# Attention output with both pairs' left-over keys first, GpSimd waits on VectorE, and a plan with other durations

## The chip, the cores and the metric

One core of a Trainium2 chip runs the whole kernel. The metric is the device time of one execution in microseconds (us), as the median of several runs. Engine names are those of the profile: PE (TensorE), PEld (its weight loads), DVE (VectorE), ACT (ScalarE), POOL (GpSimd), SP (SyncE, which issues the DMAs).

## What is computed

For 8 batches, 12 heads, 448 positions and a head width of 64, attention with normalized queries and keys, then a gated MLP on the heads laid side by side:

```python
q_n, k_n = rmsnorm(q, g_q), rmsnorm(k, g_k)
scores = q_n @ k_n.T / sqrt(64)
attn = exp(scores - max) ; attn /= sum + 1e-9
x = (attn @ v) laid out as (8, 448, 768)
h = gelu(x @ w_in)                  # 768 -> 1024, u and v halves of 512
v_n = layernorm(v) * g_ln
v_s = w_sg @ v_n + b_sg             # over the 448 positions
out = x + (u * v_s) @ w_out         # 512 -> 768
```

Inputs are float32; the kernel splits most operands into a high and a low 16-bit half (names ending in `h` and `l`) and adds three products of halves for each product.

## The kernel before

**The work.** Two heads are a pair, two pairs (`NG = 2`, index `j`) are a unit `u`; there are 24 units, three to a batch. For a unit, `split` (L740) normalizes queries and keys on POOL, DVE and ACT (tiles `qk`, `hl`) and a transposing DMA makes `qt`. `scores` (L793) forms seven score tiles `s`, each of 12 matmuls in 64x64 weight tiles; DVE takes the row extremum (`jk`), ACT the exponential (`ex`), ACT or DVE the two halves (`ahl`), and a transposing DMA writes them to `at`. [...]

**The attention output** is `pv` (L855). It runs twice per unit (`e = 0, 1`: four and three of the unit's seven query chunks), 48 times in all, and adds into one PSUM tile `pv`. 448 keys are three whole chunks of 128 and a left-over of 64. `steps` (L859) lists both: the left-over keys take two weight tiles of 64x64, a whole chunk two tiles of 128x64. With the three products of halves this makes 12 blocks per pair, and `blocks` is ordered with the three left-over blocks first. The loop runs over the pairs outside and the blocks inside, so that the left-over blocks of pair 1 come after the whole chunks of pair 0, and it yields after block 5 of each pair and after pair 0. `recips` (L828) takes the reciprocals of the sums on POOL and DVE (`rx`, `ry`, `rh`, `rl`), `rows` (L839) spreads them by matmuls of 128x64, and DVE multiplies.

**The MLP** (`moe`, L905) uses whole 128x128 weight tiles (`mv`, `mu`, `ms`, `mo`); its instructions are recorded with an offset `MOFF` in their priority.

**What sets the order.** No engine call is made directly. A `Tape` records each as a task with a priority (the place in which it was recorded, plus an offset), a duration from `cost` (L127) and what it depends on. On PE consecutive matmuls of one output tile and one weight-tile shape are one task, and a `yield` cuts a task. `schedule` (L247) then plans all engines together in time, an available task with the lowest priority number first; for PE it charges a change of the weight-tile shape (`SWITCH`) and may prefer a task of the present shape that is up to `HYST` places later. [...] Some tasks may go to either of two engines (`either`, L226). `emit` (L403) writes the tasks in the planned order of start, so each engine's queue has that order; at run time the engines wait for data and buffers alone. All instructions are issued on L425, so the profile tells them apart by tile.

Of the kernel before, what the change touches and what calls it, by code (L numbers as in the profile page):

```python
# [15 lines left out]
ALU = mybir.AluOpType  # L16
# [5 lines left out]
LEAST = 1.125 * 2.0 ** -15  # L22
ASC = 2.0 ** 14


MOFF, MOFF0, GP = 340, 100, 350

HI, EL, LO, SQ, QH, QL, RW, XH, OT, GH, VH = "A", "VA", "V", "A", "AV", "G", "A", "A", "A", "A", "A"

# [22 lines left out]
SWITCH, HYST = (133, 92), 160  # L52
BIAS = dict(A=0, V=0, G=0)
SLACK = (0, 0)
OVER, PATIENCE = dict(V=130, G=150), 300
START = dict(T=60, A=34, V=33, G=85, S=28, N=0)


class Tile:
# [37 lines left out]
class Tape:  # L97

    def __init__(self, tc):
        self.tc, self.tiles, self.tasks, self.off, self.count = tc, {}, [], 0, 0  # L100
        self.after = set()
        self.grouped = self.last = None
        self.masks, self.swap = {}, None

    def free(self, ap):
        n = 1
# [20 lines left out]
    def cost(self, q, op, a, kw):  # L127

        aps = [x for x in kw.values() if isinstance(x, bass.AP)]
        n = max([self.free(x) for x in aps], default=1)  # L130
        wide = [k for k in ("in_", "in0", "in1") if k in kw and self.free(kw[k]) > max(n // 2, 1)]
        psum = any(self.tiles[kw[k].tensor.name].pool.space for k in wide if kw[k].tensor.name in self.tiles)
        if q.eng == "T":
            t, big = kw["lhsT"], kw["rhs"]
            rows, cols = (64 if ap_n <= 64 else 128 for ap_n in (t.shape[0], self.free(t)))
            m = self.free(big)
            d = max(m / 2.4, 26.7 if cols == 64 else 53)
            if big.dtype == F32R:
                d = max(d, 186)
            if big.dtype == F32:  # L140
                d = max(4 * m / 2.4, 250)
            return d * rows * cols / 128 ** 2 + (4 if rows == cols == 128 else 3), 170, (rows, cols)
        if q.eng != "S" and "dma" in op:
            return 700, 4000, None
        if q.eng == "S":
            b = n * kw["out"].shape[0] * mybir.dt.size(kw["out"].dtype)
            if "transpose" in op:
                return 1530, b / 458752, True
            return 600, b / 220e3, False
        if "preload" in op:  # L150
            return 1283, 0, None
        if q.eng == "A":
            ptr = sum(isinstance(kw.get(k), bass.AP) for k in ("bias", "scale"))
            return 0.833 * n + (70 if psum else 100) + 80 * ptr + (200 if "accum_out" in kw else 0), 100, None
        if q.eng == "V":
            if op == "reciprocal":
                return 70 + 6.5 * n, 75, None
            ptr = sum(isinstance(kw.get(k), bass.AP) for k in ("scalar", "scalar1", "scalar2"))
            one = len(wide) == 1 and not psum and "reduce" not in op and "bn" not in op
            f32 = one and (mybir.dt.size(kw[wide[0]].dtype) == 4 or kw[wide[0]].dtype == U16)  # L160
            return (0.52 if f32 else 1.04) * n + 75 + 40 * ptr + (70 if "accum_out" in kw else 0), 75, None
        if n < 100:
            return 1.5 * n + 185, 20, None
        wide = [k for k in wide if len([x for x in kw[k].ap if x[0]]) == len(kw[k].ap)]
        return (1.86 if len(wide) > 1 else 2.5 if op == "tensor_scalar" else 1.64) * n + 210, 20, None

    def port(self, q, op, kw):

        if q.eng == "G":
            return True  # L170
        if q.eng != "V" or max(self.free(v) for v in kw.values() if isinstance(v, bass.AP)) < 16 or op not in ("tensor_tensor", "scalar_tensor_tensor", "tensor_scalar", "tensor_copy"):
            return False
        aps = [v for v in kw.values() if isinstance(v, bass.AP) and v.tensor.name in self.tiles]
        return not any(self.tiles[v.tensor.name].pool.space for v in aps)
# [72 lines left out]
    def schedule(self):  # L247
# [42 lines left out]
        T = self.tasks  # L290
# [7 lines left out]
        free = dict.fromkeys(START, 0.0)  # L298
# [7 lines left out]
        mode, dma, left, now, port = None, (0.0, False), len(T), 0.0, 0.0  # L306
        while left:
            moved = True
            let_go()
            while moved:  # L310
                moved = False
                for e in START:
# [5 lines left out]
                    t, put = None, []  # L318
                    while avail[e] and t is None:
# [6 lines left out]
                        shared = T[k].alts[e][3] if T[k].alts else T[k].port  # L326
# [4 lines left out]
                        t = T[k]  # L331
                    if e == "T" and t is not None and t.mode != mode:
                        same = [x for x in avail[e] if T[x[1]].mode == mode and x[0] < t.prio + HYST and opens(T[x[1]], now)]
                        if same:
                            x = min(same)
# [3 lines left out]
                            t = T[x[1]]  # L339
# [19 lines left out]
                    if t.port:  # L359
                        over = min(OVER[e], occ / 2)  # L360
                        port = max(port, now + over) + occ - over
# [4 lines left out]
                    end = free[e] + t.lat  # L366
                    if e == "S":
                        z, x = t.lat, max(0.0, dma[0] - now)
                        if t.mode:
                            occ += min(1350, max(0, 0.85 * (x - 1750)))  # L370
                            end = max(now + 2500 + 1550 * z, min(now + 3000 + 1750 * z, dma[0] + 2400 * z), dma[0] + 1520 * z)
                        else:
                            occ += 450 * (dma[1] and x > 2000)
                            end = max(now + 2500 + 400 * z, dma[0] + (1000 if dma[1] else 500) + 400 * z)
# [8 lines left out]
                            heapq.heappush(events, tl.end)  # L383
                    for s in succ[t.id]:
                        f = T[s].eng
                        r = free[e] + 15 if f == e and not T[s].alts else end + START[f]
                        ready[s] = max(ready[s], r)
                        need[s] -= 1
                        if not need[s]:
                            for f in T[s].alts or (f,):  # L390
                                heapq.heappush(later[f], (ready[s], s))
                            heapq.heappush(events, ready[s])
# [10 lines left out]
    def emit(self, real_pools):  # L403
        tc = self.tc

        def real(v):
            tl = self.tiles.get(v.tensor.name) if isinstance(v, bass.AP) else None
            if tl is None:
                return v
            if tl.real is None:  # L410
                shape, dtype = tl.args
                tl.kw.pop("kind", None)
                tl.real = real_pools[tl.pool.name].tile(list(shape), dtype, **tl.kw)
            r = tl.real if v.dtype == tl.real.dtype else tl.real.bitcast(v.dtype)
            return bass.AP(tensor=r.tensor, offset=v.offset, ap=v.ap)

        for t in self.schedule():
            for c in t.calls:
                if t.eng == "N":
                    real_pools["swap"]()  # L420
                    continue
                q, op, a, kw = c
                kw = {k: real(v) for k, v in kw.items()}
                first = (kw.pop("out"),) if op == "memset" else ()
                getattr(q.nc_eng, op)(*first, *a, **kw)  # L425


@with_exitstack
def kernel(
# [15 lines left out]
    B, H, S, D = q.shape  # L445
# [8 lines left out]
    HP = P // 2  # L454
# [5 lines left out]
    NG = 2  # L460
# [17 lines left out]
    V, A, G = nc.vector, nc.scalar, nc.gpsimd  # L478
# [25 lines left out]
    T, A, V, G, SP = (Queue(tape, e, x) for e, x in zip("TAVGS", (nc.tensor, nc.scalar, nc.vector, nc.gpsimd, nc.sync)))  # L504
    mm = T.matmul
# [56 lines left out]
    def decode(dst, raw, most=None):  # L562

        hi, lo = raw[:, :, 1], raw[:, :, 0]
        di = dst.bitcast(I32)
        V.tensor_scalar(out=di, in0=hi, scalar1=0x7FFFFFFF, scalar2=None, op0=ALU.bitwise_and)
        if most is None:
            V.tensor_scalar(out=dst, in0=dst, scalar1=LEAST, scalar2=None, op0=ALU.max)
        else:
            V.tensor_scalar(out=dst, in0=dst, scalar1=LEAST, scalar2=None, op0=ALU.max, op1=ALU.max, accum_out=most)  # L570
        V.tensor_scalar(out=di, in0=di, scalar1=3, scalar2=0x3FFFFFF8, op0=ALU.logical_shift_left, op1=ALU.bitwise_and)
        V.scalar_tensor_tensor(out=di, in0=hi, scalar=-0x40000000, in1=di, op0=ALU.bitwise_and, op1=ALU.bitwise_or)
        V.scalar_tensor_tensor(out=di, in0=lo, scalar=29, in1=di, op0=ALU.logical_shift_right, op1=ALU.bitwise_or)
# [107 lines left out]
    R, U = {}, {}  # L681
# [173 lines left out]
    def pv(u, e):  # L855
        n = C4 - e
        at = U[u]["at"][e]
        av = at.rearrange("p x (c j q) -> p x j c q", j=NG, q=HP)
# [5 lines left out]
        yield  # L864
        ps = ps_m.tile([P, 512], F32, name="pv", tag="pv")[:, 0:n * P]
        pc = ps.rearrange("p (c j q) -> p j c q", j=NG, q=HP)
        for j in range(NG):
            r = R[NG * u + j]
            for k_, (v_, o, hx) in enumerate(blocks):
                for h, (ks, c) in enumerate(hx):  # L870
                    mm(out=pc[h * HP:(h + 1) * HP, j], lhsT=r[v_][ks, c], rhs=av[ks, o + c, j, 0:n],
                       start=(j == 0 and k_ == 0), stop=(j == NG - 1 and k_ == len(blocks) - 1), skip_group_check=True)
                if k_ == 5:
                    yield
            if j == 0:
                yield
        if ROWP:
            row = rows(e, *r_)
# [260 lines left out]
    for i in range(NI + 1):  # L1139
        b, g = divmod(i, NP)  # L1140
        u = i // NG
# [92 lines left out]
```

## Time and profile before

| | |
|---|---|
| median of 3 runs | 884.81 us (882.46 to 885.58) |
| the profiled execution, its own time | 881.78 us |
| its span, first to last instruction | 880.0 us |
| busy: PE / PEld / DVE / ACT / POOL | 766.3 / 456.0 / 685.8 / 727.9 / 317.6 us |
| mean granted TensorE clock | 0.957 |

A profile's row for a group names the line, the engine, the instruction, output and input tiles, and how many there are. In a timeline the time from one matmul's start to the next one's is what a matmul occupies PE for; the durations beside them overlap, because matmuls are pipelined.

### The profile page before, as it was taken

To read this page: it belongs to the slowest core of one execution; us is meant where nothing else is said; L and a number is where in the kernel's file an instruction comes from. 1 tells how busy PE (TensorE), PEld (TensorE's weight loads), DVE (VectorE), ACT (ScalarE), POOL (GpSimd) and SP (SyncE) were. 2 spreads that over 40 slices of the span, in tenths; PEclk is the share of its full clock that TensorE was granted. 3 is DMA by queue.
4 is the path that set the end of the run, shared out by engine and by line. 5 is a ranking of instruction groups with operands and counts; after the bars stand their busy time and mean duration, and the time that the engine had idled before them with its cause. 6 is when DMAs were issued, how large, how long until landed. Compare 5 with 4: busy or idle time off the path is not lost.

```text
span 880.0 us, 20978 instructions
## 1 busy us (share of the span) xinstructions
PE 766.3 (87%) x7766; PEld 456.0 (52%) x7766; DVE 685.8 (78%) x1690; ACT 727.9 (83%) x1495; POOL 317.6 (36%) x458
## 2 busy tenths in 40 slices
PE   0445669547999999999999999999999999999997
PEld 0222334223574467544754477456745575457457
DVE  6899997998887987868877979688887978583150
ACT  4779789987988998989999989799999978884351
POOL 3554520274453344535433506542553341000000
PEclk9997869856999999999999999999999999999999
DMA  6999989889899959998999599969999698635002
GB/s 161 262 256 233 227 178 216 162 187 215 167 221 227 204 116 217 231 199 167 188 221 219 129 215 188 226 157 180 210 226 175 124 183 178 147 85 100 19 1 72
DMA packets 433942, 155.96 MB, mean 177 GB/s; under 512 B 402544, under 2 KB 427696, under 8 KB 433840
## 3 DMA queue, kind: packets, MB, share of 16 engines
q1 hardware_dynamic: 433840, 154.63, 85.8%
q8 instruction: 61, 1.00, 0.5%
q14 instruction: 41, 0.34, 0.1%
HBM read 43.57 MB, written 11.01 MB: 62 GB/s over the span
## 4 chain that ended last, share of the span: by engine, by line
PE 56%; DVE 18%; ACT 14%; issue 5%; DMA 3%; POOL 2%; SPq 0%; ACTq 0%; DVEq 0%; POOLq 0%
PE pv L425 11%; PE s L425 8%; DVE jk L425 4%; ACT ex L425 3%; DVE dec L425 3%; ACT ahl L425 3%; ACT L425 2%; PE row L425 2%; DMA at<-ahl 2%; DVE vl L425 1%; DVE ahl L425 1%; DVE ss L425 1%; ACT u L425 1%; POOL qk L425 1%; ACT sqk L425 1%
## 5 line engine op out<-in xcount | busy, mean ns | idle before, releaser
L425 ACT ACTIVATE ex<-s,nm 128x448 int32<-128x448 f32 x336 | 212.3, 634 | 29.8 <-DVE jk L425 25.3
L425 DVE TENSOR_SCALAR_CACHE_REDUCE jk<-s 128x448 bf16<-128x448 f32 x336 | 199.5, 617 | 43.5 <-PE s L425 42.6
L425 PE MATMUL s<-qt 64*64 64x448 f16 x2016 | 148.3, 383 | 79.7 <-ACT ex L425 58.1
L425 ACT ACTIVATE ahl<-ex 128x896 f16<-128x896 uint16 x191 | 179.7, 952 | 8.5 <-DMA at<-ahl 7.8
L425 PEld LDWEIGHTS <-vh 128*64 128x64 f16 (+2 forms) x1792 | 100.5, 111 | 89.7 <-issue 64.0
L425 PE MATMUL pv<-at,vh 128*64 128x256 f16 (+3 forms) x1536 | 140.8, 274 | 5.7 <-DMA at<-ahl 3.1
L425 PEld LDWEIGHTS <-qt 64*64 64x64 f16 x2016 | 62.5, 111 | 117.9 <-issue 76.7
L425 DVE TENSOR_SCALAR ahl<-ex 128x896 f16<-128x896 uint16 x145 | 103.7, 716 | 25.0 <-ACT ex L425 20.7
L425 POOL TENSOR_TENSOR hl<-qk,hl 128x896 f16<-128x896 f32 (+2 forms) x69 | 97.2, 1419 | 21.1 <-DVE hl L425 13.4
L425 POOL TENSOR_SCALAR rx<-sums 128x8 f32<-128x8 f32 (+1 forms) x48 | 16.5, 344 | 213.6 <-ACT ex L425 212.2
L425 POOL TENSOR_TENSOR qk<-qk,ny 128x896 f32<-128x896 f32 x47 | 83.1, 1787 | 1.8
L425 PEld LDWEIGHTS <-wi 128*128 128x128 f16 x576 | 52.0, 98 | 53.0 <-issue 7.7
L425 PE MATMUL pv<-at,vl 128*64 128x192 f16 (+3 forms) x768 | 74.4, 274 | 0.0
L425 PEld LDWEIGHTS <-vl 128*64 128x64 f16 (+2 forms) x896 | 49.3, 110 | 45.0 <-issue 27.7
L425 PEld LDWEIGHTS <-xh 128*128 128x128 f16 (+1 forms) x648 | 48.8, 103 | 42.9 <-issue 18.8
L425 POOL TENSOR_TENSOR qk<-qk,gg 128x896 f32<-128x896 f32 x23 | 48.4, 2106 | 60.3 <-ACT sqk L425 57.2
L425 ACT ACTIVATION_READ_ACCUMULATOR ex<-s,nm 128x1 f32 x336 | 69.0, 205 | 0.0
L425 DVE TENSOR_TENSOR pv<-pv,row 128x512 f32<-128x512 f32 (+1 forms) x48 | 30.2, 629 | 39.5 <-PE pv L425 39.3
L425 DVE TENSOR_REDUCE ss<-sqk 128x14 f32<-128x896 f32 x48 | 51.7, 1079 | 9.2 <-ACT sqk L425 9.1
L425 ACT ACTIVATE sqk<-qk 128x896 f32<-128x896 f32 x48 | 45.7, 954 | 2.9 <-DMA qk<-in_k_dram 1.5
L425 PEld LDWEIGHTS <-xl 128*128 128x128 f16 (+1 forms) x408 | 36.6, 103 | 20.4 <-issue 1.7
L425 ACT ACT_TABLE_LOAD x36 | 46.2, 1283 | 0.6
(1104 smaller groups left out, 1797.7 us busy)
## 6 DMA issues: line engine op xcount, KB each, us to landing
qk<-in_q_dram SPq DMA_DIRECT2D x48, 224.0 KB, 3.8
qk<-in_k_dram SPq DMA_DIRECT2D x48, 224.0 KB, 4.6
out_dram<-ot SPq DMA_DIRECT2D x56, 192.0 KB, 3.2
raw<-in_moe_w_in_dram SPq DMA_DIRECT2D x12, 512.0 KB, 5.3
vr<-in_v_dram SPq DMA_DIRECT2D x32, 192.0 KB, 3.6
vr<-in_v_dram SPq DMA_DIRECT2D x32, 144.0 KB, 3.6
rawo<-in_moe_w_out_dram SPq DMA_DIRECT2D x8, 384.0 KB, 4.0
at<-ahl SPq DMA_TRANSPOSE x168, 4.2
```

What stands on the lines that cost most here:

```text
L425: getattr(q.nc_eng, op)(*first, *a, **kw)
```

## The change

- In `pv` the left-over blocks of both pairs come first (6 blocks), then the whole chunks of pair 0 and of pair 1 (9 blocks each). One loop over the 24 blocks takes the place of two; it yields after blocks 5 and 14 (`CUTS`) and so once less.
- `emit` keeps the last DVE instruction with `port` set. A POOL instruction whose planned duration is over 500 ns (`LONG`) is made to wait for it.
- The plan gets other durations: ACT and DVE constants by some ns, no fast rate for a DVE instruction that also accumulates, and no shared port for it; DVE's latency 85 for 75; between dependent POOL instructions 85 ns for 15 (`AGAIN`). `MOFF` is 300 for 340.
- `decode` is rewritten to record the same instructions.

```diff
-MOFF, MOFF0, GP = 340, 100, 350
+MOFF, MOFF0, GP = 300, 100, 350
+LONG = 500
+CUTS = (5,14)
+CA = 200
+CV = 70
+AG = 85
+AGAIN = dict(T=15, A=15, V=15, G=AG, S=15, N=15)
@@ cost
-            return 0.833 * n + (70 if psum else 100) + 80 * ptr + (200 if "accum_out" in kw else 0), 100, None
+            return 0.833 * n + (52 if psum else 95) + 85 * ptr + (CA if "accum_out" in kw else 0), 100, None
-            one = len(wide) == 1 and not psum and "reduce" not in op and "bn" not in op
+            one = len(wide) == 1 and not psum and "reduce" not in op and "bn" not in op and "accum_out" not in kw
-            return (0.52 if f32 else 1.04) * n + 75 + 40 * ptr + (70 if "accum_out" in kw else 0), 75, None
+            return (0.52 if f32 else 1.04) * n + 70 + 50 * ptr + (CV if "accum_out" in kw else 0), 85, None
@@ schedule
-                        r = free[e] + 15 if f == e and not T[s].alts else end + START[f]
+                        r = free[e] + AGAIN[e] if f == e and not T[s].alts else end + START[f]
@@ emit
-                getattr(q.nc_eng, op)(*first, *a, **kw)
+                ins = getattr(q.nc_eng, op)(*first, *a, **kw)
+                if t.port and q.eng == "V":
+                    holder = ins
+                elif t.port and holder is not None and t.occ > LONG:
+                    tc.add_manual_dep(ins.ins, holder.ins.name, self.behind, reason="shared port")
@@ pv
-        for j in range(NG):
-            r = R[NG * u + j]
-            for k_, (v_, o, hx) in enumerate(blocks):
-                for h, (ks, c) in enumerate(hx):
-                    mm(out=pc[h * HP:(h + 1) * HP, j], lhsT=r[v_][ks, c], rhs=av[ks, o + c, j, 0:n],
-                       start=(j == 0 and k_ == 0), stop=(j == NG - 1 and k_ == len(blocks) - 1), skip_group_check=True)
-                if k_ == 5:
-                    yield
-            if j == 0:
+        steps = [(j, x) for part in (blocks[:3], blocks[3:]) for j in range(NG) for x in part]
+        for k_, (j, (v_, o, hx)) in enumerate(steps):
+            for h, (ks, c) in enumerate(hx):
+                mm(out=pc[h * HP:(h + 1) * HP, j], lhsT=R[NG * u + j][v_][ks, c], rhs=av[ks, o + c, j, 0:n],
+                   start=(k_ == 0), stop=(k_ == len(steps) - 1), skip_group_check=True)
+            if k_ in CUTS:
                 yield
```

**PE, one `pv` tile (the 22nd of 48) before.** `ms` and `mo` are MLP tiles (128x128), `s` a score tile (64x64); `vh_5211`, `vl_5263` are the two halves of pair 0's values, `vh_5281`, `vl_5295` those of pair 1. One row stands for two matmuls (left-over) or for six (whole chunks, 12 for `s`).

```order
L425 MATMUL ms__6124<-ws_h_105,vl_5951 128x448
...
L425 MATMUL pv_6136<-at1_5759,vh_5211 64x3x64
...
L425 MATMUL pv_6136<-at1_5759,vl_5263 64x3x64
...
L425 MATMUL pv_6136<-at1_5759,vh_5211 64x3x64
...
L425 MATMUL ms__6124<-ws_h_105,vh_5945 128x448
...
L425 MATMUL pv_6136<-at1_5759,vh_5211 64x3x64
...
L425 MATMUL pv_6136<-at1_5759,vl_5263 64x3x64
...
L425 MATMUL s_6181<-qt_5232 64x448
...
L425 MATMUL pv_6136<-at1_5759,vh_5281 64x3x64
...
L425 MATMUL pv_6136<-at1_5759,vl_5295 64x3x64
...
L425 MATMUL ms__6206<-ws_h_105,vh_5945 128x448
...
L425 MATMUL pv_6136<-at1_5759,vh_5281 64x3x64
```

Each pair has its own piece of left-over matmuls, and each pair's whole chunks come apart from them.

**The same tile in the change.** Here `vh_5152`, `vl_5180` are pair 0's and `vh_5211`, `vl_5284` pair 1's.

```order
L433 MATMUL ms__6081<-ws_h_105,vl_5940 128x448
...
L433 MATMUL pv_6094<-at1_5807,vh_5152 64x3x64
...
L433 MATMUL pv_6094<-at1_5807,vl_5180 64x3x64
...
L433 MATMUL pv_6094<-at1_5807,vh_5152 64x3x64
...
L433 MATMUL pv_6094<-at1_5807,vh_5211 64x3x64
...
L433 MATMUL pv_6094<-at1_5807,vl_5284 64x3x64
...
L433 MATMUL ms__6081<-ws_h_105,vh_5901 128x448
...
L433 MATMUL pv_6094<-at1_5807,vh_5152 64x3x64
...
L433 MATMUL pv_6094<-at1_5807,vl_5180 64x3x64
...
L433 MATMUL s_6145<-qt_5373 64x448
...
L433 MATMUL pv_6094<-at1_5807,vh_5211 64x3x64
...
L433 MATMUL ms__6185<-ws_h_105,vh_5901 128x448
```

The left-over blocks of both pairs are now one piece of 12 matmuls, and each pair's 18 whole-chunk matmuls stand together; `pv` appears in three pieces where it had five. Over the whole program the shape of the weight tile changes 421 times between one matmul and the next, where it changed 606 times; from the 577th of the 2016 score matmuls on it is 329 for 476.

**POOL, the queries and keys of one unit before,** with the semaphores that each waits for (`DVE_49` is VectorE's).

```order
L425 TENSOR_TENSOR qk_4268<-qk_4268,gg_112 128x896 [waits DMAHW4_49,DMAHW3_49,Activation_49]
...
L425 TENSOR_TENSOR qk_4268<-qk_4268,ny_4968 128x896 [waits DMAHW2_49,DMAHW1_49,Pool_49]
L425 TENSOR_TENSOR qk_4268<-qk_4268,ny_4968 128x896
L425 TENSOR_SCALAR rx_5093<-sums_4813 128x8 [waits Activation_49]
L425 CAST rh_5131<-ry_5118 128x8 [waits DVE_49,PE_49]
L425 TENSOR_TENSOR rl_5133<-ry_5118,rh_5131 128x8 [waits PE_49,Pool_49]
L425 TENSOR_TENSOR hl_5135<-qk_4268,hl_5135 128x2x7x64 [waits DMAHW5_49,DVE_49]
L425 TENSOR_TENSOR hl_5137<-qk_4268,hl_5137 128x2x4x64 [waits DMAHW7_49,Activation_49]
L425 TENSOR_TENSOR hl_5137<-qk_4268,hl_5137 128x2x3x64 [waits DVE_49]
```

Of these wide instructions two wait for DVE.

**The same unit in the change.**

```order
L433 TENSOR_TENSOR qk_4328<-qk_4328,gg_112 128x896 [waits DMAHW4_49,DMAHW5_49,DVE_49,Activation_49]
...
L433 TENSOR_TENSOR qk_4328<-qk_4328,ny_4865 128x896 [waits DMAHW2_49,DMAHW3_49,DVE_49,Pool_49]
L433 TENSOR_TENSOR qk_4328<-qk_4328,ny_4865 128x896 [waits DVE_49]
L433 TENSOR_TENSOR hl_4979<-qk_4328,hl_4979 128x2x7x64 [waits DMAHW6_49,DVE_49,Pool_49]
L433 TENSOR_TENSOR hl_5031<-qk_4328,hl_5031 128x2x4x64 [waits DVE_49]
L433 TENSOR_TENSOR hl_5031<-qk_4328,hl_5031 128x2x3x64 [waits DVE_49,Activation_49]
L433 TENSOR_SCALAR rx_5133<-sums_4886 128x8 [waits Activation_49]
L433 CAST rh_5150<-ry_5145 128x8 [waits DVE_49,PE_49]
L433 TENSOR_TENSOR rl_5154<-ry_5145,rh_5150 128x8 [waits PE_49,Pool_49]
```

Now all of the wide instructions on `qk` and `hl` wait for DVE, and the small `rx`, `rh`, `rl` that `rows` needs stand behind them in the queue. In the whole program 96 of the 138 wide ones wait for DVE, where 31 of 139 did; one multiplication by `ny` has moved to DVE. Casts `hl<-qk` on ACT are 34 where they were 40, on DVE 38 for 32.

## Rows read from the trace of the kernel before

**Rows 1.** The page: busy time by engine, then the span in 40 slices.

```profile
PE 766.3 (87%) x7766; PEld 456.0 (52%) x7766; DVE 685.8 (78%) x1690; ACT 727.9 (83%) x1495; POOL 317.6 (36%) x458
...
PE   0445669547999999999999999999999999999997
...
PEclk9997869856999999999999999999999999999999
```

**Rows 2.** Three stretches: PE, PEld, DVE, ACT, POOL busy; granted clock, DMA share, GB/s.

```profile
0.00:220.00 220.00, 122.90 (x1232) 64.47 (x1232) 196.80 (x461) 178.94 (x352) 89.00 (x123) 0.83 0.98 210
220.00:880.00 660.00, 643.39 (x6542) 391.56 (x6534) 489.02 (x1230) 548.97 (x1143) 228.63 (x335) 1.00 0.82 166
385.00:440.00 55.00, 53.19 (x526) 33.08 (x525) 47.90 (x120) 52.65 (x109) 23.89 (x34) 1.00 0.93 177
```

**Rows 3.** Waits of PE from 220 to 880 us: total us, times, longest.

```profile
PE s L425 <- ACT ex L425: 4.7, 7, 1.0
PE row L425 <- DVE xl L425: 3.1, 5, 1.1
PE pv L425 <- ACT row L425: 2.2, 3, 0.7
```

**Rows 4.** Timeline of PE, 411 to 417 us: start us, us, matmuls.

```profile
411.56 0.27 PE L425 MATMUL pv<-at,vh 64*64 64x192 f16 x2
411.76 0.36 PE L425 MATMUL ms__6124<-ws_h,vh 128*128 128x448 f16 x1
...
412.53 0.35 PE L425 MATMUL ms__6124<-ws_l,vh 128*128 128x448 f16 x1
412.72 0.35 PE L425 MATMUL ms__6124<-ws_h,vl 128*128 128x448 f16 x1
413.00 0.44 PE L425 MATMUL pv<-at,vh 128*64 128x192 f16 x6
413.27 0.41 PE L425 MATMUL pv<-at,vl 128*64 128x192 f16 x6
413.52 0.41 PE L425 MATMUL pv<-at,vh 128*64 128x192 f16 x6
413.90 0.76 PE L425 MATMUL s<-qt 64*64 64x448 f16 x12
414.46 0.28 PE L425 MATMUL pv<-at,vh 64*64 64x192 f16 x2
```

**Rows 5.** DVE groups from 0 to 220 us: busy us, mean ns; idle before.

```profile
L425 DVE TENSOR_SCALAR ahl<-ex 128x896 f16<-128x896 uint16 x21 | 17.2, 821 | 1.2 <-ACT ex L425 1.2
...
L425 DVE SCALAR_TENSOR_TENSOR wr<-rawo,wr 128x384 int32<-128x384 int32 x16 | 12.6, 789 | 0.0
```

**Rows 6.** Timeline of DVE, then of POOL, 191 to 196 us.

```profile
191.52 0.62 DVE L425 TENSOR_SCALAR ahl<-ex 128x896 f16<-128x896 uint16 x1
192.05 2.43 DVE L425 SCALAR_TENSOR_TENSOR wr<-rawo,wr 128x384 int32<-128x384 int32 x1
...
195.94 0.55 DVE L425 SCALAR_TENSOR_TENSOR wr<-rawo,wr 128x384 int32<-128x384 int32 x1
...
191.97 2.10 POOL L425 TENSOR_TENSOR qk<-qk,gg 128x896 f32<-128x896 f32 x1 [1.31 <-ACT sqk L425]
```

**Rows 7.** The chain of waits, 130 to 230 us: start us, us, what.

```profile
192.14 2.34 DVE wr L425
...
197.78 3.73 POOL qk L425 x2
...
214.10 3.43 DVE vl L425 x3
```

**Rows 8.** Timeline of POOL, 394 to 397 us.

```profile
394.36 0.19 POOL L425 CAST rh<-ry 128x6 f16<-128x6 f32 x1
394.51 2.08 POOL L425 TENSOR_TENSOR qk<-qk,gg 128x896 f32<-128x896 f32 x1
396.55 0.38 POOL L425 TENSOR_TENSOR rl<-ry,rh 128x6 f16<-128x6 f32 x1
```

More of the change, by code (lines that the diff above doesn't have):

```diff
@@ L103, in __init__ @@
         self.masks, self.swap = {}, None
+        self.behind = mybir.DependencyInfo(mybir.DependencyClass.Sync, mybir.DependencyReason.SCHED_ONLY)
     def free(self, ap):
@@ L170, in port @@
             return True
-        if q.eng != "V" or max(self.free(v) for v in kw.values() if isinstance(v, bass.AP)) < 16 or op not in ("tensor_tensor", "scalar_tensor_tensor", "tensor_scalar", "tensor_copy"):
+        if q.eng != "V" or "accum_out" in kw or max(self.free(v) for v in kw.values() if isinstance(v, bass.AP)) < 16 or op not in ("tensor_tensor", "scalar_tensor_tensor", "tensor_scalar", "tensor_copy"):
             return False
@@ L415, in real @@
             return bass.AP(tensor=r.tensor, offset=v.offset, ap=v.ap)
+        holder = None
         for t in self.schedule():
@@ L566, in decode @@
         V.tensor_scalar(out=di, in0=hi, scalar1=0x7FFFFFFF, scalar2=None, op0=ALU.bitwise_and)
[L567 to L570, printed above, removed]
+        more = {} if most is None else dict(op1=ALU.max, accum_out=most)
+        V.tensor_scalar(out=dst, in0=dst, scalar1=LEAST, scalar2=None, op0=ALU.max, **more)
         V.tensor_scalar(out=di, in0=di, scalar1=3, scalar2=0x3FFFFFF8, op0=ALU.logical_shift_left, op1=ALU.bitwise_and)
```

## The prediction

> **What bounds the kernel now.** I read the page first, for which engine is full and where. PE is busy 766.3 us of 880, and by slices it has two parts: the first ten slices (to 220 us) are ragged, with a granted clock down to 0.5 in one of them; from 220 us on PE stands at 9 in every slice but the last, at full clock [rows 1]. The windows say the same in us: PE is busy 122.9 of the first 220 us, but 643.4 of the last 660 [rows 2]. A busy PE need not be a useful one, because the ends of matmuls are modelled, so the third view is what PE waits for after 220 us: six entries that come to 12.0 us, the largest of them 4.7 us for ACT's exponentials [rows 3]. POOL is not among them. So for three quarters of the span what PE does one after another is the time. The next engine is ACT: 549.0 of these 660 us, and in the fullest stretch that I looked at 52.7 of 55 us beside PE's 53.2 [rows 2]. Before 220 us the chain goes mainly through DVE and ACT, and DVE is busy 196.8 of 220 us [rows 2].
>
> The fourth view, PE's timeline, shows the price that matters. Inside one shape of weight tile the 128x128 matmuls start 0.19 us apart (412.53 to 412.72); the step from there to `pv`'s 128x64 takes 0.28 us (412.72 to 413.00), 0.09 more. Six whole-chunk matmuls take 0.25 us when the next six have their shape (413.27 to 413.52) and 0.38 us when a score tile of 64x64 follows (413.52 to 413.90), 0.13 more. Coming out of the left-over matmuls into the MLP takes 0.20 us (411.56 to 411.76) where such a pair goes by in about 0.08, 0.12 more. From scores to left-over matmuls, the same shape, a score tile takes just its 0.56 us (413.90 to 414.46) [rows 4]. So a change of shape costs PE 0.09 to 0.13 us; I take 0.11, the middle.
>
> **The change part by part.**
>
> *Order in `pv`.* It removes no matmul. It joins pieces: per `pv` tile one left-over piece for two, and fewer cuts through the whole chunks. The two orders shown above give 606 changes of shape before and 421 now. Of the 185 that go, 38 lie before the 577th score matmul (about 262 us in the profile), where PE is mostly not the bound, and 147 behind it, where it is. 147 x 0.11 = 16.2 us saved; with the two ends of the price 13.2 and 19.1. The 38 early ones (4 us of PE's time) I cost at nothing: the cover is DVE's work, and if that cover is thinner than it looks they add up to 4 us of gain.
>
> *What must keep up.* Joined pieces are longer: a `pv` piece of 18 matmuls takes about 0.8 us (three rows of six), and the order now puts two score tiles one behind the other more often. Both PSUM buffers for scores must then be free at once, or PE stands until ACT has read them. PE waited 4.7 us for that after 220 us [rows 3]. PE also asks for all else 2.5% faster, 16 of 660 us; ACT goes from 549.0 in 660 to about 549 in 644 us, 83% to 85%, less 6 casts that moved to DVE. I add 2 us for waits that come back; the bounds are 0 and 12, which doubles [rows 3].
>
> *GpSimd's waits.* [...] DVE's `wr` took 2.43 us at 192.05 and 0.55 us at 195.94; POOL's multiplication by `gg` had begun at 191.97 and took 2.10 us [rows 6]. DVE lost 1.9 us there, POOL nothing. To 220 us the halves `ahl` average 821 ns on DVE against 0.62 us for one that was not held up, `wr` 789 against 550 [rows 5, 6]: 21 x 0.20 + 16 x 0.24 = 8 us in two forms. Two such stalls lie on the chain itself, the `wr` of 2.34 us and three `vl` of 3.43 us [rows 7], which at 0.55 and 3 x 0.6 would have been 3.4 us less. The new waits let POOL start only behind the DVE instruction that the plan put ahead of it, so some of these stalls go. I take 2 us, near the chain's 3.4 because only stalls on the chain count, and half of it because a held-up DVE instruction that the plan puts behind POOL's is still held up. The gain is bounded by the 8 us of the two forms. The loss: the chain has a POOL piece too, two multiplications of 3.73 us [rows 7]; each can now wait for a DVE instruction of 0.6 us, and a few of those are 2 us. After 220 us I cost the waits at nothing: POOL is busy 228.6 of 660 us and PE's matmuls wait for it nowhere [rows 2, 3].
>
> [...]
>
> *Durations and `MOFF`.* They move work by places, not in amount. One multiplication goes from POOL to DVE at the very start, where both contended anyway. I cost them at nothing; what covers it is that PE's queue holds the same work in nearly the same sequence of units. If a bad place arises it shows as a PE wait, within the 12 us above.
>
> **Sum.** Against the profiled execution's own 881.8 us (span 880.0 and 1.8 around it): 881.8 - 16.2 + 2 - 2 = 865.6, taken as **866 us**. The median of the runs shown stands 3.0 us above the profiled one; carried over to it, the same sum would be 868.6, well within the range.
>
> **The rivals.**
>
> *ACT takes over.* For: in 385 to 440 us it is busy 52.7 of 55 us [rows 2], so there a faster PE finds no scores to work on, and double score tiles bunch its work. Against: over 660 us it has 111 us to spare, and PE's waits for it are short. If half of the stretches give nothing, half of 16.2 is lost: 881.8 - 8.1 + 2 - 2 = 874.
>
> [...]
>
> [...]
>
> *The reciprocals come late (slower).* `rh` and `rl` stand in POOL's queue behind wide instructions. At 394.36 `rh` was followed by a multiplication of 2.08 us, so `rl` began at 396.55 [rows 8]. If now a waiting wide instruction holds such a pair for 2.1 us and PE has nothing else, each costs 2.1 us; the point is 16.2 / 2.1 = 8 of 48 pairs. At 16 pairs the time is 881.8 - 16.2 + 33.6 - 2, about 897. Against: PE's matmuls wait for POOL nowhere after 220 us [rows 3].
>
> *Nothing in the end.* The changes of shape go, and PE waits as much more for data in other places: 880 to 886.
>
> **How the numbers follow.** Forecast (859 to 871, the lock's rival in it) 0.57, of this 0.10 for the lock's rival; ACT takes over (871 to 880) 0.17; startup gives more (848 to 859) 0.12; nothing 0.07; slower 0.07. A range of 850 to 878 holds the forecast, most of the second and third, 0.80 or so; it takes in both ends of the price (863 and 869) and 12 us of waits (876). A measurement of this kernel can tell about 0.5% from no change, that is 4.4 us. Faster by more (under 880.4): 0.57 + 0.17 + 0.12 = 0.86; within: 0.07; slower: 0.07.
>
> **What would show it.** In the profile of the changed kernel, PE's timeline at the same `pv` tile has one left-over piece of 12 matmuls and two of 18, with the starts otherwise at the same pace; PE's waits after 220 us stay near 12 us; the part behind the 577th score matmul is some 16 us shorter. [...] Wrong: PE's waits for `ex`, `rh` or `rl` grow by 10 us or more (ACT or the reciprocals), or 220 us is reached later than now (POOL on the path). If PE's steps at a change of shape stay but their count doesn't pay, the bound was not PE.

## The result

The changed kernel takes **863.14 us** (median of 5 runs, 862.73 to 863.76), the kernel before 882.46 us in the same comparison (881.17 to 885.58): a ratio of 0.977, 95% interval 0.975 to 0.979, 19 us less. The forecast was 866, range 850 to 878. The profiled execution of the changed kernel took 863.8 us (span 862.0), that of the kernel before 881.8; the sum of the forecast against it was 865.6.

The profile after. First the page, busy time and the slices, the answer to [rows 1]:

```profile
PE 745.1 (86%) x7766; PEld 468.1 (54%) x7766; DVE 669.7 (78%) x1696; ACT 721.0 (84%) x1490; POOL 308.6 (36%) x457
...
PE   0445658835999999999999999999999999999997
...
PEclk9998768965999999999999999999999999999999
```

PE is full from the eleventh slice on as before and busy 21.2 us less in all; the granted clock falls below full between the fourth and the tenth slice in both. The windows, columns as in [rows 2]:

```profile
0.00:220.00 220.00, 118.23 (x1235) 67.30 (x1236) 191.71 (x467) 175.24 (x346) 82.57 (x122) 0.83 0.97 206
220.00:862.00 642.00, 626.86 (x6533) 400.80 (x6531) 477.96 (x1230) 545.74 (x1145) 226.03 (x336) 1.00 0.87 173
385.00:440.00 55.00, 54.63 (x599) 36.79 (x597) 44.44 (x115) 51.72 (x115) 20.18 (x32) 1.00 0.90 170
```

PE stays the bound of the long part: it is busy 626.9 of 642.0 us. ACT is at 545.7 of 642.0 (85%), as worked out ahead. PE's waits in that part, as [rows 3]:

```profile
PE s L433 <- ACT ex L433: 4.5, 6, 1.1
PE pv L433 <- ACT row L433: 1.8, 4, 0.7
PE row L433 <- DVE gtl L433: 0.7, 1, 0.7
...
PE row L433 <- POOL rh L433: 0.5, 1, 0.5
```

All ten entries come to 10.1 us, before it was 12.0. The timeline of PE at the `pv` tile whose order stands above, the answer to [rows 4]:

```profile
403.77 0.35 PE L433 MATMUL ms__6081<-ws_l,vh 128*128 128x448 f16 x1
403.96 0.35 PE L433 MATMUL ms__6081<-ws_h,vl 128*128 128x448 f16 x1
404.24 0.27 PE L433 MATMUL pv<-at,vh 64*64 64x192 f16 x2
404.35 0.25 PE L433 MATMUL pv<-at,vl 64*64 64x192 f16 x2
...
404.60 0.24 PE L433 MATMUL pv<-at,vl 64*64 64x192 f16 x2
404.68 0.25 PE L433 MATMUL pv<-at,vh 64*64 64x192 f16 x2
404.86 0.36 PE L433 MATMUL ms__6081<-ws_h,vh 128*128 128x448 f16 x1
...
406.37 0.41 PE L433 MATMUL pv<-at,vl 128*64 128x192 f16 x6
406.61 0.41 PE L433 MATMUL pv<-at,vh 128*64 128x192 f16 x6
406.96 0.76 PE L433 MATMUL s<-qt 64*64 64x448 f16 x12
```

The 12 left-over matmuls are one piece: 0.62 us from its first start to the next MLP matmul (404.24 to 404.86). The steps at a change of shape are what they were: 0.28 us into the piece (403.96 to 404.24) where the pace is 0.19, and 0.35 us for six whole-chunk matmuls ahead of a score tile (406.61 to 406.96) where the six before took 0.24. Only their number fell.

The same price comes out of all of PE's order, and it goes with the shape and not with the cut. I took pieces (consecutive matmuls of one tile and one shape) in the long part, from the first mark of the table below on, and for each the time to the next piece's start less its streaming time, as defined there. In the kernel before the median is 0.135 us at the 502 places where the shape changes and 0.026 us at the 361 places where another tile of the same shape follows; in the changed kernel it is 0.141 us (349) and 0.026 us (326). In these two kernels a cut between pieces of one shape takes 0.026 us; a change of shape takes 0.11 us more.

On DVE beside POOL, the two groups of [rows 5] in the first 220 us:

```profile
L433 DVE TENSOR_SCALAR ahl<-ex 128x896 f16<-128x896 uint16 x22 | 16.2, 734 | 1.8 <-DMA at<-ahl 1.7
...
L433 DVE SCALAR_TENSOR_TENSOR wr<-rawo,wr 128x384 int32<-128x384 int32 x16 | 11.4, 724 | 0.0
```

821 ns became 734 and 789 became 724, where single ones that were not held up took 620 and 550 in [rows 6]: the stalls are fewer, far from gone. In the chain of waits, the answer to [rows 7], the three `vl` that took 3.43 us now take 1.54:

```profile
200.44 1.70 POOL qk L433
...
215.87 1.54 DVE vl L433 x3
```

**One table for all runs.** It is worked out from each trace, PE's matmuls in order of start. Each is given a streaming time in proportion to its columns and to the elements of its weight tile, by which a score tile of 12 gets the 0.56 us of [rows 4], six whole-chunk matmuls 0.24 (406.37 to 406.61), and a 128x128 matmul with 448 columns 0.187, where the timeline's pace is 0.19. A pair of left-over matmuls gets 0.04 where it takes 0.08 (404.60 to 404.68); what is over counts as steps, for the same matmuls in every kernel. The first column is the instant at which 80 us of streaming have started, a fixed amount of work near the end of the ragged part; the second is the rest of the span, with 538 us of streaming in each kernel. What is left of the rest is split: the time from a matmul's start to the next one's, less its streaming time, is added to the steps where it is at most 0.35 us (changes of shape and small losses) and to the gaps where it is more (PE waits). The 5 us that are left follow the last matmul. Medians are of all executions; the other columns are of one profiled execution each. The executions of one kernel spread over 1 us (the changed kernel) to 8 us (run 3), so 1 or 2 us at the first mark show nothing by themselves.

| kernel | runs, median us | to 80 us of streaming | rest | changes of shape in the rest | steps | gaps |
|---|---|---|---|---|---|---|
| before | 882.5 | 227.9 | 652.1 | 502 | 93.5 | 15.7 |
| changed | 863.1 | 226.9 | 635.1 | 349 | 77.4 | 14.7 |
| 1 pv alone | 862.3 | 226.2 | 635.3 | 346 | 76.7 | 15.6 |
| 2 old pv | 875.3 | 227.2 | 645.2 | 494 | 95.4 | 6.4 |
| 3 no waits | 868.7 | 234.3 | 636.1 | 349 | 78.1 | 15.1 |
| 4 waits alone | 876.3 | 226.1 | 649.6 | 502 | 94.0 | 12.7 |
| 5 plan alone | 882.3 | 232.5 | 646.8 | 494 | 94.4 | 9.4 |
| 6 more cuts | 865.8 | 226.6 | 637.4 | 398 | 84.0 | 10.4 |
| 7 pairs, one cut | 862.4 | 225.6 | 634.9 | 386 | 81.5 | 10.5 |
| 8 one cut, joined | 868.9 | 225.8 | 641.4 | 297 | 73.9 | 24.4 |
| 9 pv and waits | 865.1 | 228.4 | 634.7 | 346 | 76.5 | 15.1 |
| 10 old MOFF | 861.9 | 224.1 | 635.1 | 350 | 77.0 | 15.1 |
| 11 all POOL waits | 866.3 | 226.9 | 637.7 | 349 | 78.5 | 16.2 |
| 12 one cut and waits | 870.1 | 227.2 | 642.5 | 376 | 81.3 | 18.2 |

Between the first two rows: 153 changes of shape fewer and 16.1 us less in steps, 0.105 us each; 1.0 us less in gaps and 1.0 us earlier at the first mark. That is the 18 us between the two spans. Over all fourteen rows a straight line through steps against changes of shape has a slope of 0.109 us per change and leaves a scatter of 0.9 us.

By the mark that the forecast named, the 577th score matmul, the part behind it went from 618.3 to 599.8 us, and the mark itself from 261.7 to 262.1: nothing was won ahead of it that one execution could show.

### The profile page after: what moved, and what is told of

Its sections match the earlier page's. It is cut to its first block, busy times and chain, and to the rows that moved or that the text cites. A ratio compares the mean times of both kernels' runs of the same rounds, so it can differ in the third digit from the quotient of the medians.

```text
span 862.0 us, 20985 instructions
## 1 busy us (share of the span) xinstructions
PE 745.1 (86%) x7766; PEld 468.1 (54%) x7766; DVE 669.7 (78%) x1696; ACT 721.0 (84%) x1490; POOL 308.6 (36%) x457
## 4 chain that ended last, share of the span: by engine, by line
PE 43%; ACT 22%; DVE 20%; issue 6%; DMA 5%; POOL 2%; SPq 0%; ACTq 0%; DVEq 0%; POOLq 0%
PE pv L433 8%; PE s L433 6%; ACT ex L433 6%; DVE jk L433 4%; ACT ahl L433 4%; DMA at<-ahl 3%; ACT L433 3%; DVE dec L433 2%; DVE ahl L433 2%; DVE wr L433 2%; DVE ss L433 2%; DVE vl L433 2%; ACT u L433 2%; ACT vh L433 2%; PE row L433 1%
## 5 line engine op out<-in xcount | busy, mean ns | idle before, releaser
L433 PE MATMUL s<-qt 64*64 64x448 f16 x2016 | 141.8, 382 | 77.7 <-ACT ex L433 56.3
L433 PE MATMUL pv<-at,vh 128*64 128x192 f16 (+3 forms) x1536 | 132.3, 274 | 7.6 <-DMA at<-ahl 5.6
L433 POOL TENSOR_TENSOR hl<-qk,hl 128x512 f16<-128x512 f32 (+2 forms) x69 | 92.0, 1343 | 50.0 <-issue 17.1
L433 POOL TENSOR_TENSOR qk<-qk,ny 128x896 f32<-128x896 f32 x46 | 78.0, 1705 | 15.6 <-DVE ahl L433 3.5
L433 PEld LDWEIGHTS <-wi 128*128 128x128 f16 x576 | 54.6, 99 | 53.0 <-issue 5.8
L433 PEld LDWEIGHTS <-vl 128*64 128x64 f16 (+2 forms) x896 | 55.7, 113 | 16.9 <-DVE vl L433 4.5
L433 DVE TENSOR_REDUCE ss<-sqk 128x14 f32<-128x896 f32 x48 | 51.7, 1080 | 10.5 <-ACT sqk L433 10.5
```

The costliest lines, as they stand in the source:

```text
L433: ins = getattr(q.nc_eng, op)(*first, *a, **kw)
```

## The experiments

Each was timed against the kernel before on the same chip; that kernel's median was 882.8 to 883.7 us in the three groups (runs 1 to 4, 5 to 8, 9 to 12). Ratios are to it, with 95% intervals. Two runs whose intervals overlap are not clearly apart: this holds for the 2 to 3 us by which runs 6, 9 and 11 lie above the change. The theory: PE's changes of shape pay for nearly all. The rivals: the waits or the durations carry a good part; or the order of the pairs does it, not the count of changes. The lock is the forecast's name for DVE being held up beside POOL, as in [rows 6] (2.43 us for 0.55); no run shows what holds it up.

**1. The new `pv` alone.** The kernel before with this loop and its cuts:

```diff
-        for j in range(NG):
...
+        steps = [(j, x) for part in (blocks[:3], blocks[3:]) for j in range(NG) for x in part]
...
+            if k_ in CUTS:
                 yield
```

> The kernel before with the new order and cuts in pv alone; no GpSimd waits, the old durations and MOFF. Its PE order has 421 changes of weight-tile shape (before 606), 147 of the 185 fewer ones behind the 577th score matmul. Theory A (PE's changes of shape at 0.11 us each pay for nearly all): 882.5 - 16 = 866 (863 to 869). Theory B (the waits and the durations carry a good part): 872 or more. Theory C (it is the plan that had to be right for joined pieces, so alone they bring waits for scores): over 875.

862.25 us, ratio 0.976 (0.973 to 0.978): as fast as the whole change. In the table all but 1.7 us of it lies in the rest, 16.8 us, and that in the steps. Theory A holds; its 866 (863 to 869) was a little high. The waits, durations and `MOFF` together add nothing to it that the times show.

**2. The whole change but for `pv`.**

```diff
-        steps = [(j, x) for part in (blocks[:3], blocks[3:]) for j in range(NG) for x in part]
...
+        for j in range(NG):
...
+                if k_ == 5:
+                    yield
+            if j == 0:
                 yield
```

> The changed kernel with the old loop in pv (pairs outside, its three cuts); GpSimd waits, durations and MOFF stay. 592 changes of shape, 329 + 133 = 462 behind the 577th score matmul. Theory A: 863.1 + 133 x 0.11 = 878 (875 to 881). Theory B: under 872.

875.3 us, ratio 0.991 (0.989 to 0.994). The steps are back (95.4 us), but the gaps fell to 6.4. So on the new durations and waits `pv` is worth 12 us by the runs, at the lower edge of theory A's range: 18.0 us of steps, of which 8.3 us return as gaps.

**3. The change without GpSimd's waits.**

```diff
-LONG = 500
+LONG = 1e9
```

> The changed kernel without GpSimd's waits; the order on every engine is the same. Forecast's theory: DVE is held up again in the first 220 us, 2 us more: 865 (863 to 867). Rival (the lock only changes sides, POOL loses what DVE gains): 863, no difference. Rival (the waits cost on the path of the reciprocals): under 862.

868.7 us, ratio 0.984 (0.980 to 0.987), 5.6 us over the changed kernel with the same order on every engine. The table puts it in the first part, 234.3 for 226.9; but the profiled execution took 872.2 us, of six that took 864.5 to 872.6 (the changed kernel's five: 862.7 to 863.8), so these 7.4 us are more than the usual loss. It comes in steps, the two largest at DVE instructions that a multiplication on POOL holds up. Timelines of this run, DVE and then POOL, at these two:

```profile
108.02 2.53 DVE L433 SCALAR_TENSOR_TENSOR dec<-raw,dec 128x512 int32<-128x512 int32 x1
...
107.91 2.08 POOL L433 TENSOR_TENSOR qk<-qk,gg 128x896 f32<-128x896 f32 x1 [9.29 <-ACT sqk L433]
...
186.14 2.17 DVE L433 TENSOR_SCALAR wr<-wr 128x384 int32<-128x384 int32 x2
188.24 2.04 DVE L433 SCALAR_TENSOR_TENSOR wr<-rawo,wr 128x384 int32<-128x384 int32 x1
...
186.41 3.45 POOL L433 TENSOR_TENSOR qk<-qk,ny 128x896 f32<-128x896 f32 x2
```

and the same instructions in the changed kernel, where POOL's rows name the DVE instruction that they waited for:

```profile
105.58 0.68 DVE L433 SCALAR_TENSOR_TENSOR dec<-raw,dec 128x512 int32<-128x512 int32 x1
...
106.93 2.07 POOL L433 TENSOR_TENSOR qk<-qk,gg 128x896 f32<-128x896 f32 x1 [9.42 <-DVE ahl L433]
...
180.16 0.71 DVE L433 TENSOR_SCALAR wr<-wr 128x384 int32<-128x384 int32 x2
180.79 0.55 DVE L433 SCALAR_TENSOR_TENSOR wr<-rawo,wr 128x384 int32<-128x384 int32 x1
...
181.75 1.69 POOL L433 TENSOR_TENSOR qk<-qk,ny 128x896 f32<-128x896 f32 x1 [1.10 <-DVE wr L433]
183.94 1.69 POOL L433 TENSOR_TENSOR qk<-qk,ny 128x896 f32<-128x896 f32 x1 [0.49 <-DVE wr L433]
```

`dec` takes 2.53 us for 0.68 where POOL's multiplication began 0.11 us ahead of it and took 2.08 us; the `wr` instructions at 186.14 and 188.24 take 2.17 and 2.04 us for 0.71 and 0.55. In the changed kernel POOL starts behind them and runs its own 2.07 and 1.69 us without loss. The forecast's 2 us was low. Nor did POOL lose what DVE gained: against the first row of this run's page, DVE is busy 8.4 us less in the changed kernel (669.7 us, in the result above) and POOL 6.7 us less (308.6).

```profile
PE 749.1 (86%) x7766; PEld 470.0 (54%) x7766; DVE 678.1 (78%) x1696; ACT 721.4 (83%) x1490; POOL 315.3 (36%) x457
```

**4. The waits alone,** with the order of the kernel before:

```diff
+                ins = getattr(q.nc_eng, op)(*first, *a, **kw)
+                if t.port and q.eng == "V":
+                    holder = ins
+                elif t.port and holder is not None and t.occ > LONG:
+                    tc.add_manual_dep(ins.ins, holder.ins.name, self.behind, reason="shared port")
```

> The kernel before with GpSimd's waits alone; the order on every engine is the same as before. Forecast's theory: 2 us less, 880.5 (878 to 882). Rival (changes sides): 882.5. In the profile the mean of ahl on DVE in the first 220 us falls from 821 ns towards 620 ns either way.

876.3 us, ratio 0.992 (0.989 to 0.994): 6.8 us less, more than either theory had. By the spans it is 4.3 us: 1.8 before the mark, 2.5 behind it, where I had costed the waits at nothing. The sign that I had named failed: the mean of `ahl` in the first 220 us is 807 ns, hardly less than 821, and `wr<-rawo,wr` went from 789 to 739. The gain is spread over other instructions: over the whole span DVE is busy 8.6 us less than before (677.2 for 685.8) and POOL 6.8 (310.8 for 317.6).

```profile
PE 761.3 (87%) x7766; PEld 452.5 (52%) x7766; DVE 677.2 (77%) x1690; ACT 728.2 (83%) x1495; POOL 310.8 (35%) x458
```

**5. Durations and `MOFF` alone.**

```diff
-MOFF, MOFF0, GP = 340, 100, 350
+MOFF, MOFF0, GP = 300, 100, 350
...
-                        r = free[e] + 15 if f == e and not T[s].alts else end + START[f]
+                        r = free[e] + AGAIN[e] if f == e and not T[s].alts else end + START[f]
```

(and the lines of `cost` and `port`)

> The kernel before with the new durations and MOFF alone: old loop in pv, no GpSimd waits. 592 changes of shape, 14 fewer than before and all of those fewer ones early or spread. Theory A (shape changes are the price): 881 to 882.5. Theory B (better durations give an order in which PE waits less): 878 or under.

882.3 us, ratio 0.998 (0.996 to 1.000). The sum is nothing, the parts are not: the first mark comes 4.6 us later, the gaps behind it are 6.3 us less.

**6. More cuts.**

```diff
-CUTS = (5,14)
+CUTS = (5,8,14,17)
```

> The changed kernel with cuts after blocks 5, 8, 14 and 17: the left-over blocks of both pairs stay joined, the whole chunks are cut into pieces of 3 and 6 blocks as in the kernel before. 482 changes of shape, 377 behind the 577th score matmul for 329. Theory A: 863.1 + 48 x 0.11 = 868.4 (866 to 870). Rival (the joined left-over blocks are what counts, since a left-over piece alone is short): 863 to 864.

865.8 us, ratio 0.979 (0.977 to 0.982). 49 more changes of shape cost 6.6 us of steps, 0.135 each, and the gaps fall by 4.3. Against the change the runs lie 2.7 us up, between the two theories.

**7. Pairs outside again, one cut.** The old loop in the changed kernel, without its cuts after block 5:

```diff
-                if k_ == 5:
-                    yield
             if j == 0:
                 yield
```

> The changed kernel with the pairs outside again, but one cut only, between the pairs: left-over 3 and whole 9 blocks of pair 0, then of pair 1. 474 changes of shape, 362 behind the 577th score matmul for 329. Theory A: 863.1 + 33 x 0.11 = 866.7 (865 to 869): most of the gain comes from fewer cuts, not from the order of the pairs. Rival (the order of the pairs is the gain): 873 or more.

862.4 us, ratio 0.976 (0.974 to 0.978), level with the change. 37 more changes of shape cost 4.1 us of steps, and 4.2 us fewer gaps pay for them. So with these durations the order of the pairs is not needed for the gain; fewer cuts do as well. Both theories missed the number, the rival by more.

**8. One cut only, behind the left-over blocks.**

```diff
-CUTS = (5,14)
+CUTS = (5,)
```

> The changed kernel with one cut only, behind the left-over blocks: the 18 whole-chunk blocks of both pairs, 36 matmuls, are one piece. 360 changes of shape, 279 behind the 577th score matmul for 329. Theory A: 863.1 - 50 x 0.11 = 857.6 (855 to 860). Rival (a piece of 1.6 us holds up the scores, and PE then waits for ACT and ACT for PE): 863 or more, with more waits of DVE's jk for scores.

868.9 us, ratio 0.984 (0.982 to 0.987): slower than the change. The steps fall by 3.5 us, and the gaps rise by 9.7. Theory A fails here. The rival's time is right, and so is its sign, more waits of DVE's `jk` for scores: 37.4 us, 27.3 in the changed kernel in the same part. But PE's own waits are not where it put them. From 226 us on they,

```profile
PE ms__7662 L433 <- ACT vh L433: 3.9, 1, 3.9
PE pv L433 <- DMA at<-ahl: 3.8, 3, 1.7
PE row L433 <- DVE gtl L433: 2.2, 1, 2.2
PE s L433 <- ACT ex L433: 2.0, 4, 0.8
```

are for the MLP's halves and for `at`, `gtl`; those for ACT's exponentials are short. The longer pieces made others late; which of them PE then meets is the plan's affair.

A part of the loss is the clock. Behind 226 us the changed kernel has the full granted clock (1.00) to its last matmul; this run (0.99 over that part) has three stretches at half of it, 10 us in all, from 319.8, 487.1 and 592.9 us on; before them PE had waited 1.3, 3.9 and 2.2 us. The second one, first in a row of the windows (columns as in [rows 2], the clock is 0.50), then in PE's timeline:

```profile
487.10:490.50 3.40, 3.11 (x9) 1.19 (x10) 1.63 (x3) 3.40 (x9) 0.24 (x1) 0.50 0.79 229
...
483.11 0.35 PE L433 MATMUL ms__7662<-ws_h,vl 128*128 128x448 f16 x1
487.39 0.56 PE L433 MATMUL ms__7662<-ws_h,vh 128*128 128x448 f16 x1 [3.93 <-ACT vh L433]
...
488.12 0.58 PE L433 MATMUL ms__7662<-ws_h,vl 128*128 128x448 f16 x1
488.49 0.58 PE L433 MATMUL ms__7673<-ws_h,vh 128*128 128x448 f16 x1
...
490.80 0.35 PE L433 MATMUL ms__7662<-ws_l,vh 128*128 128x448 f16 x1
490.99 0.35 PE L433 MATMUL ms__7662<-ws_h,vl 128*128 128x448 f16 x1
```

The pace is 0.37 us (488.12 to 488.49) where at full clock it is 0.19 (490.80 to 490.99). The three stretches hold 4.5 us of the steps; at the changed kernel's rate (77.4 us in 635) it would be 1.2. So by this estimate some 3 us of the loss are the clock's, and without them the steps would have fallen by about 7 us for 52 changes. The rows suggest that the waits brought the lower clock, so that a wait of PE cost more than its own length; no run tests this.

**9. `pv` and waits, old durations and `MOFF`** (the edits of 1 and 4 together, against the kernel before):

```diff
+        steps = [(j, x) for part in (blocks[:3], blocks[3:]) for j in range(NG) for x in part]
...
+                    tc.add_manual_dep(ins.ins, holder.ins.name, self.behind, reason="shared port")
```

> The kernel before with the new pv and GpSimd's waits, old durations and MOFF: the change without its third part. 421 changes of shape. pv alone gave 862.3 and the waits alone 6.8 less than before. Theory D (the new durations only cost, in the first 230 us, and the waits are worth 2 us early and some PE waits later on any plan): 858 (856 to 860), faster than the changed kernel. Theory E (the waits only mend what a plan has that doesn't fit, and the new pv has already taken that): 862 to 863.

865.1 us, ratio 0.980 (0.977 to 0.982). Neither: the waits, worth 6.8 us on the old order, here give nothing; the median is 2.9 us over run 1, with intervals that overlap slightly. The rest is the same (634.7 us, 635.3 in run 1); the first mark is 2.2 us later than without them. What the waits give depends on the order that they guard, and DVE's busy time tells the orders apart. The rows of run 1 and of this run:

```profile
PE 744.2 (86%) x7766; PEld 467.7 (54%) x7766; DVE 670.6 (78%) x1690; ACT 726.0 (84%) x1495; POOL 319.0 (37%) x458
...
PE 743.9 (86%) x7766; PEld 468.1 (54%) x7766; DVE 669.9 (78%) x1690; ACT 726.3 (84%) x1495; POOL 314.6 (36%) x458
```

Here the waits take 0.7 us off DVE's busy time; where they gained 5.6 to 7 us of the kernel's time (run 3 to the change, run 4, run 5 to run 2) they took off 8.4 to 9.4.

**10. The change with the old `MOFF`.**

```diff
-MOFF, MOFF0, GP = 300, 100, 350
+MOFF, MOFF0, GP = 340, 100, 350
```

> The changed kernel with MOFF at 340 as before: 422 changes of shape, new durations and waits. If the cost of the third part sits in MOFF: 857 to 860. If it sits in the durations, or there is none beside the waits: 862 to 864.

861.9 us, ratio 0.976 (0.973 to 0.978): the interval takes in the change's 0.977. `MOFF` is worth nothing that these runs can tell.

**11. All of POOL waits.**

```diff
-LONG = 500
+LONG = 0
```

> The changed kernel with LONG = 0: GpSimd's small instructions (norms, reciprocals) wait for DVE's last port instruction too, 245 rows of its queue wait for DVE where 178 did; the same order on every engine. The rival of the late reciprocals: each of 48 pairs rh, rl waits up to 0.6 us and PE with it, 863.1 + up to 29 us; over 867 if a quarter of that shows. Theory A: PE has other work queued, 863 to 865, and PE's waits for rh and rl stay under 3 us after 226 us.

866.3 us, ratio 0.980 (0.978 to 0.983), 3.2 us over the change and between the two cases. PE waits 1.5 us in all for `rh` and `rl` from 226 us on. The reciprocals have room; the rival that ended slower needed far more. What the 3.2 us are, if they are real, stays open.

**12. Old order of the pairs, one cut, waits, old durations** (the edit of 4, and in `pv` of the kernel before):

```diff
-                if k_ == 5:
-                    yield
             if j == 0:
                 yield
```

> The kernel before with the pairs outside as they were, one cut only (between the pairs), and GpSimd's waits; old durations and MOFF. 468 changes of shape, 360 behind the 577th score matmul for 346 with the new order of the pairs. If the order of the pairs is worth nothing beside the number of changes and PE's waits: within 2 us of the kernel with the new pv and waits. If the order of the pairs matters by itself: 5 us or more above it.

870.1 us, ratio 0.986 (0.983 to 0.988), 4.9 us over run 9, the edge of the second case. By the table it has 4.8 us more in steps and 3.1 in gaps, and is 1.2 earlier at the mark. Of the steps 1.7 us lie in a stretch at half clock from 324.8 us on, behind a PE wait of 3.3 us; no other run but 8 has one in the long part. With run 7, which lost nothing to the new order of the pairs, the order by itself stays open: its worth changes with the plan.

No version beats the changed kernel beyond the intervals; runs 1, 7 and 10 stand level with it.

## Why the prediction was right, point by point

**PE is the bound from 220 us on: right.** Streaming and steps fill it, gaps are 15 of 635 us. Each kernel with the new `pv` and its two cuts has a rest of 634.7 to 637.7 us (the change, 1, 3, 9, 10, 11), whatever the durations, `MOFF` or waits are.

**16.2 us for 147 changes of shape: right.** The table gives 16.1 us in steps for 153 behind its mark (a little earlier than the 577th score matmul), 0.105 us each where I took 0.11 from a few steps of one timeline. What the kernel's time makes of it goes with the order around it: 20.9 us in run 1, 12.2 from run 2 to the change.

**2 us for waits that come back: wrong in sign, by 3 us.** Gaps went from 15.7 to 14.7. But the trade that I named is real: joined further (run 8) they reach 24.4, with more cuts (run 6) 10.4, with the old loop on the new durations 6.4.

**The early changes of shape at nothing: not contradicted.** 32 fewer of them before the mark; it came 1.0 us earlier, within the spread of executions.

**Startup 2 us less by the waits, durations at nothing: the sum was near (1.0) by luck, both terms were off and nearly cancelled.** In the profiled executions the durations alone put the first mark 4.6 us later (run 5), and on the new `pv` 8.1 us later (run 3 against run 1; 6.5 us by the medians); on these two orders the waits take back 5.3 (run 2 against 5; 7.0 by the medians) and 7.4 us (the change against 3; 5.6 by the medians). With the old durations they take 1.8 (run 4) or add 2.2 (run 9 against 1). The step that failed is "I cost them at nothing; what covers it is that PE's queue holds the same work": in the first part PE is not the bound, so its queue covers nothing there.

**The rival in which POOL loses what DVE gains: wrong.** On the same order DVE is busy 8.4 us less with the waits and POOL 6.7 us less, and the run without them is 5.6 us slower (run 3 against the change): DVE's loss was not handed to POOL. POOL's waits for DVE went up from 158.9 us over the span in run 3 to 185.5, but its waits in all did not (500.7 and 499.5). No run shows a lock, the name that the forecast's chances use; what run 3 shows is a DVE instruction that takes longer beside POOL: `dec` at 108.02, begun 0.11 us behind POOL's multiplication, ended 0.56 us behind its end, and takes 0.68 us when not held up.

**The other rivals.** ACT did not take over: PE's waits for `ex` are 4.5 us, 4.7 before. The reciprocals cost 0.5 us. Startup gave 1 us at most, far from the 848 to 859 of its case. And PE's waits did not take back the steps, as "nothing in the end" had it: its gaps went down by 1.0 us.

**Open:** why the new durations make the first part later without the waits. The runs show where the steps of lag are, not which of the durations brought POOL's multiplications there.

## What to carry to other kernels

Where TensorE is full, count how often the weight tile's shape changes between one matmul and the next, price one from the timeline as a step against its neighbours, and join pieces of one shape; here 0.105 us times 153 was 16.1 of the 18.0 us between the spans. Joining has an end: in run 8 longer pieces gave it back as waits (24.4 us of gaps for 14.7), so measure one step further as well. A wait that keeps a GpSimd multiplication behind the VectorE instruction beside it must be judged on the very order that it guards; it was worth from 7 us gained to nothing, perhaps 3 us lost, here. DVE's busy time with and without it shows whether there was anything to win.

## What was not expected of the hardware

A small DVE instruction was held up beside POOL as well, of a size that the kernel's own `port` (16 elements and up) leaves out of the plan. In the run without waits, DVE and then POOL, and the same instruction in the changed kernel:

```profile
119.21 1.60 DVE L433 SCALAR_TENSOR_TENSOR wi_part<-wi_part,wi_up 128x6 int32<-128x6 int32 x1
...
119.10 1.69 POOL L433 TENSOR_TENSOR qk<-qk,ny 128x896 f32<-128x896 f32 x1
```

```profile
115.08 0.15 DVE L433 SCALAR_TENSOR_TENSOR wi_part<-wi_part,wi_up 128x6 int32<-128x6 int32 x1
```

Six elements per partition took 1.60 us for 0.15, nearly as long as the multiplication beside it (1.69 us).
